# The last batch's division on ScalarE, a shorter guard, and a new order, in a fused attention and MLP kernel on one core

## The chip, the core and the metric

The kernel runs on one NeuronCore of a Trainium2 chip. TensorE (PE, with its weight load PEld), VectorE (DVE), ScalarE (ACT), GpSimd (POOL) and SyncE (SP) each work through an instruction list of their own and wait for one another by semaphores. SP issues all transfers between HBM and SBUF; 16 DMA engines carry them, called the wire below. The metric is the device time of one execution, in microseconds (us).

## The reference

`x` has 4 batches of 12480 rows of 128 numbers, all in float32. A set of 32 inducing rows attends to each batch, each batch then attends to the 32 rows that came of it, and every row goes through a layer with the activation h - tanh(h).

```python
def mab(q, kv):
    s = scale * (q @ kv.transpose(0, 2, 1))
    s = s - s.max(-1, keepdims=True)
    a = np.exp(s)
    a /= a.sum(-1, keepdims=True) + 1e-09
    return a @ kv
h = mab(I, x)
return mab(x, h)
...
h = x @ w_in          # 128 -> 2048
g = h - np.tanh(h)
return g @ w_out      # 2048 -> 128
```

## The kernel before, in words

A batch is cut into steps 0 to 7 of 1536 rows and a remainder, step 8, of 192; batches are counted 0 to 3. Two passes run over each batch.

The *first pass* (`first`, L367) loads a step's `x` transposed (`xT`, L380) and makes its scores against the inducing rows on PE (L357). VectorE copies them out with their maximum (L391), ScalarE takes exponents (L461), VectorE transposes (L465), and PE sums up the weighted rows (L472). That sum needs the rows untransposed: they are loaded a second time (`xn`, L455), or, for the steps in `TURNED`, turned on PE (L447) and copied out by ScalarE or VectorE (L451). At the end of a batch its summary `hT_all` of 32 rows is made (L510).

`linear` (L519) then replaces the layer for this batch by its tangent around the mean of the 32 rows: one 32x128 matrix per batch, `P_all`. That holds only as long as the rows are close to one another. So a *guard* (`bound`, L699) works out whether it held: it reduces a bound r1, a bound r2 and the least denominator `smin` over all sums to one number each, PE transposes them to one partition (L754 to L756), and VectorE forms a single number, `limit`, from them (`decide`, L759, nine instructions on one-element tiles and two reductions among them). Every engine reads `limit` at the end (L846) and jumps over the long way (`general`) unless it is over zero (L847). With these inputs the long way isn't run.

The *second pass* (`second`, L612) makes the scores of a step against the summary (L357, this time with `hT_all`), their maximum (L625, L626) and exponent (L629), and the product with `P_all` in four quarters of one PSUM bank each (L636), whose last column is the denominator. VectorE copies the denominators to `S_all` (L648) and takes reciprocals (L651). Each quarter then goes out of PSUM in one of two ways: VectorE divides it on the way (`whole`, L660), or ScalarE copies it (`plain`, L664) and POOL divides it in SBUF (`norm`, L669). SP stores a step in one transfer; steps 6 and 7 of the last batch go in two halves (L695).

No loop runs in the program: `Plan.order` (L110) lays all of this out before it is built. It goes through the work in time with estimated costs, starts on each engine the ready piece with the least priority number (`K`, a table of offsets by kind and batch), and gives out places in SBUF (23 places `big` of 128x1536) and PSUM. `LAND` is its guess of a transfer's delay, `STAY` a penalty on changing PE's kind of work, `MOST` how many places each use may hold, `DVQ` how many quarters of a step start out on VectorE. What it makes is an order for each engine that the chip then keeps; SP's order is kept too, so a transfer that has to wait holds up all behind it. A transfer into a place waits until the engine that last read it is done, and each of the eight semaphores for transfers is used again only when the transfer eight before has landed.

Of the kernel before, what the change touches and what calls it, by code (L numbers as in the profile page):

```python
# [28 lines left out]
K = dict(load=(-405.2, -73.6, 365.6, 732.0), step1=(189.5, 37.3, 86.1, 34.3), lag2=(-1344.7, 642.2, -187.9, 554.4),
         copy=(-966.7, 182.8, 582.0, 890.5), step2=(63.0, 5.9, 46.9, 4.9), turn=(3399.7, 2729.3, 3806.6, 3390.1), move=(-926.9,  # L30
         616.0, 643.2, -1883.0), nat=(445.7, -196.7, -60.7, 77.0), exp1=(-409.6, -1802.6, 1772.8, 577.3), et=(-1268.2, -670.6,
         821.4, -2142.2), acc=(63.5, 1115.9, -997.2, -2667.1), sc2=(498.0, -379.7, -952.9, 693.2), top=(984.0, 131.6, 1260.3,
         -21.4), exp2=(1257.9, -709.0, 2777.2, -857.8), prod=(-1778.1, 1760.3, -578.0, -21.4), rec=(-2172.0, -394.3, 355.7,
         404.0), ev=(2492.2, -544.6, -1227.1, -3030.9), off=(-545.7, 642.1, 1621.1, 2136.7), step3=(173.1, 138.3, 60.8, 306.6),
         st=(-962.2, -256.6, 745.9, -225.9), norm=(-114.8, 1199.2, -943.7, -185.5), lw1=-186.8, lw2=25.2, w1=74.7, w2=591.6,
         bound=2765.6)
# [157 lines left out]
def fused_kernel(ctx, tc, xT, xn, xl, indT, w_in, w_out, out):  # L194
# [504 lines left out]
    def bound(pri):  # L699
# [49 lines left out]
        smin, low = small("smin", [128, 1], 1), small("low", [1, 4], 1)  # L749
        add("DVE", 0.5, lambda: nc.vector.tensor_reduce(out=smin.get(), in_=sums_all.get(), axis=AX.X, op=ALU.min),  # L750
            reads=[sums_all, *s_parts], writes=[smin], pri=pri)

        def turn():
            nc.tensor.transpose(out=ps3.get()[:1, :B], in_=r1.get(), identity=ident[:B, :B])  # L754
            nc.tensor.transpose(out=ps3.get()[:1, 128:256], in_=r2.get(), identity=ident)
            nc.tensor.transpose(out=ps3.get()[:1, 256:384], in_=smin.get(), identity=ident)  # L756
        add("PE", 0.5, turn, reads=[r1, r2, smin, ident_b], writes=[ps3], pri=pri, mode="f")

        def decide():  # L759

# [2 lines left out]
            v.tensor_reduce(out=x[:, 0:2], in_=ps3.get()[:1, 128:384].rearrange("o (k p) -> o k p", k=2), axis=AX.X, op=ALU.min)
# [1 line left out]
            v.tensor_tensor(out=x[:, 0:1], in0=x[:, 0:1], in1=x[:, 2:3], op=ALU.min)
# [1 line left out]
            v.tensor_scalar(out=x[:, 3:4], in0=x[:, 1:2], scalar1=-2.0, scalar2=2.0 * (m + SLACK), op0=ALU.mult, op1=ALU.add)
            v.tensor_tensor(out=x[:, 3:4], in0=x[:, 3:4], in1=x[:, 2:3], op=ALU.mult)
            v.tensor_tensor(out=x[:, 3:4], in0=x[:, 3:4], in1=x[:, 3:4], op=ALU.mult)
# [1 line left out]
            v.tensor_scalar(out=limit, in0=x[:, 3:4], scalar1=0.0, scalar2=None, op0=ALU.max)
# [138 lines left out]
```

## Time and profile before

| what | value |
|---|---|
| median of three runs | 188.42 us (187.48 to 188.99) |
| the profiled execution | 189.09 us |
| its span, first to last instruction | 187.2 us |
| mean granted PE clock | 0.957 |
| chain of work that ended last, by engine | PE 55%, DVE 20%, ACT 7%, DMA 6%, POOL 3% |
| bytes read from and written to HBM | 42.75 MB and 25.56 MB |

The profiled execution took 1.9 us more than its span. In the page's rows "busy" is the time in which an engine ran an instruction; the idle time before a group is followed by what ended most of it. Times in a timeline count from the span's start.

### The profile page before, as it was taken

The page shows a single profiled execution, that of the slowest core. Times are in us where ns is not written, and L with a number is a line of the kernel's source. Part 1 is how long each engine was busy: PE and PEld are TensorE (multiplying, and loading weights), DVE is VectorE, ACT ScalarE, POOL GpSimd, SP SyncE. Part 2 cuts the span into 40 slices and gives each one's busy share as a digit, 9 for nine tenths or more (in the row PEclk, how much of TensorE's full clock was granted, in tenths as well). Part 3 has the DMA queues.
Part 4 walks back from the last instruction along what each step waited for, and adds up shares of the span by engine and source line. Part 5 has one row for each costly group of instructions (what it writes and reads, how often), then busy time and mean ns, then how long its engine had stood idle before and what let it go on. Part 6 is the DMA issues. An engine that isn't in the chain of part 4 may idle for free.

```text
span 187.2 us, 7373 instructions
## 1 busy us (share of the span) xinstructions
PE 154.7 (83%) x2895; PEld 99.5 (53%) x2895; DVE 149.6 (80%) x574; ACT 112.7 (60%) x282; POOL 95.5 (51%) x114
## 2 busy tenths in 40 slices
PE   0799966879988999999999978999979988879500
PEld 0465554645345865565667864556556764646300
DVE  3268699999999987896889863599899879998950
ACT  3022389964168974756779953438589574578600
POOL 5000124672250368456755583460675886499960
PEclk9999999999999999999999995799999999999955
DMA  5999998999999999999999999699989999999991
GB/s 144 406 423 415 404 409 253 393 420 422 414 419 367 295 326 312 375 423 416 404 356 363 383 420 422 211 416 347 364 314 382 418 417 415 404 421 390 387 390 50
DMA packets 14489, 68.84 MB, mean 368 GB/s; under 512 B 1776, under 2 KB 2928, under 8 KB 14448
## 3 DMA queue, kind: packets, MB, share of 16 engines
q1 hardware_dynamic: 14448, 68.31, 94.2%
q8 instruction: 24, 0.39, 0.8%
q14 instruction: 17, 0.14, 0.2%
HBM read 42.75 MB, written 25.56 MB: 365 GB/s over the span
## 4 chain that ended last, share of the span: by engine, by line
PE 55%; DVE 20%; ACT 7%; DMA 6%; issue 5%; POOL 3%; SPq 0%; DVEq 0%; ACTq 0%; POOLq 0%
PE ps L357 17%; PE ps L636 13%; PE ps L447 10%; PE ps L472 9%; DMA big<-in_xn 3%; ACT s L461 3%; PE ps L353 3%; DMA big<-in_xT 2%; POOL big L669 2%; DVE s L391 2%; PE ps L527 2%; DVE mb L625 2%; DVE ps L327 2%; DVE big L320 2%; ACT big L323 1%
## 5 line engine op out<-in xcount | busy, mean ns | idle before, releaser
L669 POOL TENSOR_TENSOR big<-big,mb 128x384 f32<-128x384 f32 (+1 forms) x73 | 75.2, 1056 | 46.2 <-ACT big L664 41.9
L664 ACT COPY big<-ps 128x384 f32<-128x384 f32 x99 | 41.1, 488 | 8.2 <-DVE S_all L648 7.7
L636 PE MATMUL ps<-P_all,ex 32*128 32x129 f32 (+1 forms) x784 | 36.0, 294 | 4.1 <-issue 1.5
L636 PEld LDWEIGHTS ps<-P_all,ex 32*128 32x128 f32 (+1 forms) x784 | 28.1, 188 | 19.6 <-ACT big L664 5.2
L357 PE MATMUL ps<-big,indT_sb 128*32 128x384 f32 x256 | 28.1, 516 | 6.4 <-DMA big<-in_xT 6.0
L451 ACT COPY big<-ps 128x512 f32<-128x512 f32 x30 | 17.0, 587 | 25.8 <-PE ps L447 24.5
L472 PE MATMUL ps<-big,et 128*32 128x128 f32 x768 | 27.3, 275 | 5.8 <-DVE et L465 4.1
L629 ACT ACTIVATE ex<-ps,mb 128x384 f32<-128x384 f32 (+1 forms) x36 | 19.7, 553 | 17.8 <-DVE mb L626 10.8
L447 PEld LDWEIGHTS ps<-ident,big 128*128 128x128 f32 x192 | 21.6, 146 | 13.2 <-issue 4.9
L447 PE MATMUL ps<-ident,big 128*128 128x128 f32 x192 | 27.9, 290 | 0.9 <-DVE win_sb L329 0.9
L357 PE MATMUL ps<-big,hT_all 128*32 128x384 f32 x256 | 27.6, 502 | 0.2 <-DVE s L391 0.2
L472 PEld LDWEIGHTS ps<-big,et 128*32 128x32 f32 x768 | 21.0, 110 | 11.3 <-DVE et L465 5.0
L391 DVE TENSOR_SCALAR_CACHE_REDUCE s<-ps 128x384 f32<-128x384 f32 (+1 forms) x36 | 18.1, 513 | 8.8 <-PE ps L357 7.8
L461 ACT ACTIVATE s<-s,nbs 128x384 f32<-128x384 f32 (+1 forms) x36 | 21.0, 586 | 0.5 <-DVE nbs L412 0.5
L625 DVE TENSOR_REDUCE mb<-ps 128x1 f32<-128x384 f32 (+1 forms) x36 | 18.4, 511 | 2.6 <-PE ps L357 2.2
L648 DVE TENSOR_SCALAR S_all<-ps 128x3 f32<-128x3 f32 (+1 forms) x136 | 13.5, 153 | 7.3 <-PE ps L636 6.4
L465 DVE STREAM_TRANSPOSE et<-s 128x384 f32<-128x384 f32 (+1 forms) x36 | 18.1, 519 | 0.3
L660 DVE TENSOR_TENSOR big<-ps,mb 128x384 f32<-128x384 f32 x29 | 15.5, 544 | 0.3
L314 POOL TENSOR_SCALAR big<-big 128x512 f32<-128x512 f32 x8 | 5.4, 683 | 20.0 <-DMA big<-in_w_in 20.0
L451 DVE COPY big<-ps 128x512 f32<-128x512 f32 x18 | 12.3, 687 | 2.4 <-PE ps L447 2.2
L357 PEld LDWEIGHTS ps<-big,indT_sb 128*32 128x32 f32 x256 | 6.9, 113 | 12.0 <-issue 8.8
L357 PEld LDWEIGHTS ps<-big,hT_all 128*32 128x32 f32 x256 | 8.0, 111 | 5.1 <-issue 2.6
(118 smaller groups left out, 158.4 us busy)
## 6 DMA issues: line engine op xcount, KB each, us to landing
big<-in_xT SPq DMA_DIRECT2D x32, 768.0 KB, 8.8
out<-big SPq DMA_DIRECT2D x30, 768.0 KB, 7.6
big<-in_xn SPq DMA_DIRECT2D x16, 768.0 KB, 6.9
big<-in_w_in SPq DMA_DIRECT2D x4, 512.0 KB, 12.8
big<-in_w_out SPq DMA_DIRECT2D x4, 512.0 KB, 8.2
out<-big SPq DMA_DIRECT2D x4, 384.0 KB, 4.9
xr<-in_xT SPq DMA_DIRECT2D x4, 96.0 KB, 10.5
xnr<-in_xl SPq DMA_DIRECT2D x4, 96.0 KB, 7.0
```

Source lines behind the costliest of these rows:

```text
L357: nc.tensor.matmul(ps[q * m:(q + 1) * m, :sg], lhsT=w, rhs=seg(x, nq, None, q), start=True, stop=stop)
L391: nc.vector.tensor_scalar(out=s1.get()[:P, :sg], in0=ps.get()[:P, :sg], scalar1=1.0, scalar2=None, op0=ALU.mult, op1=ALU.max, accum_out=mx ...
L447: nc.tensor.transpose(out=ps.get()[:, k * 128:(k + 1) * 128], in_=xt.get()[:, c:c + 128], identity=ident)
L451: copy(x.get()[:, 4 * g:4 * g + 4, :].rearrange("p k c -> p (k c)"), ps.get())
L461: nc.scalar.activation(out=t, in_=t, func=AF.Exp, bias=nbs.get()[:P, g:g + 1], accum_out=sums.get()[:P, s:s + 1])
L465: add("DVE", 0.5 if s < NS else 0.25, lambda et=et, s1=s1s[s], P=P, sg=sg, kb=kb: nc.vector.transpose(out=et.get()[:P, :kb].rearrange("p k ...
L472: nc.tensor.matmul(hacc.get()[q * m:(q + 1) * m, g * C:(g + 1) * C], lhsT=et.get()[:P, k, :], rhs=x.get()[:P, k, :], start=first_k[g, q] = ...
L625: nc.vector.tensor_reduce(out=mb.get()[:P, 0:1], in_=ps.get()[:P, :sg], axis=AX.X, op=ALU.max)
L629: add("ACT", 0.49 if full else 0.28, lambda: nc.scalar.activation(out=ex.get()[:P, :sg], in_=ps.get()[:P, :sg], func=AF.Exp, bias=mb.get() ...
L636: nc.tensor.matmul(o_b[q].get()[:T, r * (C + 1):(r + 1) * (C + 1)], lhsT=ex.get()[p, r * T:(r + 1) * T], rhs=P_all[p, b, :], start=True, s ...
L664: nc.scalar.copy(out=slot(q, q + 1), in_=o(q)[:, :, :C])
L669: nc.gpsimd.tensor_tensor(out=x, in0=x, in1=mb.get()[:T, 2 + q0 * nr:2 + q1 * nr].unsqueeze(2).to_broadcast([T, w, C]), op=ALU.mult)
```

## The change

It has three parts.

*The last batch's steps 7 and 8.* `SCALED = 7`. A quarter of these two that goes out by ScalarE is no longer copied and divided by POOL: ScalarE multiplies by the reciprocal on the way, one instruction of 128x128 for each of a quarter's three rows of columns, since its scale is one number per partition. Any quarter of the two may go to either engine, and POOL has no `norm` for them.

*The guard.* The reduction of all sums is split: all columns but the last three products' early, into one more column of `S_all`, and the last 37 columns at the end. The transposes of r1 and r2 and their reduction to one number `c0` are pieces of work of their own. `decide` compares a multiple of the old number that needs no reciprocal and has the same sign; it keeps its scratch in PSUM, and is one reduction and four instructions with scalars in place of two reductions and seven others.

*The order.* `K`, `DVQ`, `MOST`, `LAND` and `STAY` have new numbers; `TURNED` and `GROUPS`, and so the transfers as a set, are the same.

```diff
-LEAD, AHEAD, ISSUE, LAND = 1.50, 3.00, 0.35, 1.50
-SWITCH, STAY = 0.115, 73.1
-MOST = dict(xT=15, xn=16, ot=61, pm=9)
+LEAD, AHEAD, ISSUE, LAND = 1.50, 3.00, 0.35, 1.35
+SWITCH, STAY = 0.115, 0.0
+MOST = dict(xT=15, xn=14, ot=53, pm=10)
...
-DVQ = ((2, 1, 1, 1, 2, 3, 2, 0, 1), (2, 1, 0, 2, 1, 3, 1, 2, 1), (2, 2, 0, 1, 2, 1, 1, 3, 1), (2, 1, 2, 3, 1, 2, 3, 2, 0))
+DVQ = ((1, 0, 2, 2, 2, 3, 2, 2, 1), (2, 1, 2, 2, 0, 0, 1, 2, 1), (1, 1, 2, 1, 2, 1, 2, 1, 1), (3, 1, 1, 2, 2, 1, 1, 1, 0))
+SCALED = 7
...
+        last = b == B - 1 and s >= SCALED
+        def scaled(q):
+            for r in range(nr):
+                k = q * nr + r
+                nc.scalar.activation(out=ot.get()[:T, k, :], in_=o(q)[:, r, :C], func=AF.Copy, scale=mb.get()[:T, 2 + k:3 + k])
+        if last:
+            ways["ACT"] = (0.06 + 0.28 * nr, scaled)
-            free = q >= fixed_q
+            free = q >= fixed_q or last
-        for q0, q1 in spans:
+        for q0, q1 in () if last else spans:
...
+        add("DVE", 0.5, lambda: nc.vector.tensor_reduce(out=sums_all.get()[:, B * COLS:], in_=sums_all.get()[:, :n2], axis=AX.X, op=ALU.min),
+            reads=[sums_all, *s_parts[:-3]], writes=[early], pri=pri)
+        add("DVE", 0.15, lambda: nc.vector.tensor_reduce(out=smin.get(), in_=sums_all.get()[:, n2:], axis=AX.X, op=ALU.min),
+            reads=[sums_all, early, *s_parts[-3:]], writes=[smin], pri=pri)
...
+        def room():
+            v = nc.vector
+            v.tensor_reduce(out=c0.get()[:, 0:1], in_=ps3.get()[:1, 128:256], axis=AX.X, op=ALU.min)
+            v.tensor_reduce(out=c0.get()[:, 1:2], in_=ps3.get()[:1, :B], axis=AX.X, op=ALU.min)
+            v.tensor_reduce(out=c0.get()[:, 0:1], in_=c0.get(), axis=AX.X, op=ALU.min)
...
-            v.tensor_reduce(out=x[:, 0:2], in_=ps3.get()[:1, 128:384].rearrange("o (k p) -> o k p", k=2), axis=AX.X, op=ALU.min)
-            v.tensor_reduce(out=x[:, 2:3], in_=ps3.get()[:1, :B], axis=AX.X, op=ALU.min)
-            v.tensor_tensor(out=x[:, 0:1], in0=x[:, 0:1], in1=x[:, 2:3], op=ALU.min)
-            v.reciprocal(out=x[:, 2:3], in_=x[:, 1:2])
-            v.tensor_scalar(out=x[:, 3:4], in0=x[:, 1:2], scalar1=-2.0, scalar2=2.0 * (m + SLACK), op0=ALU.mult, op1=ALU.add)
-            v.tensor_tensor(out=x[:, 3:4], in0=x[:, 3:4], in1=x[:, 2:3], op=ALU.mult)
-            v.tensor_tensor(out=x[:, 3:4], in0=x[:, 3:4], in1=x[:, 3:4], op=ALU.mult)
-            v.tensor_tensor(out=x[:, 3:4], in0=x[:, 3:4], in1=x[:, 0:1], op=ALU.subtract)
-            v.tensor_scalar(out=limit, in0=x[:, 3:4], scalar1=0.0, scalar2=None, op0=ALU.max)
+            x = ps4.get()[:1, 256:259]
+            v.tensor_reduce(out=x[:, 0:1], in_=ps4.get()[:1, :128], axis=AX.X, op=ALU.min)
+            v.tensor_scalar(out=x[:, 1:2], in0=x[:, 0:1], scalar1=-2.0, scalar2=2.0 * (m + SLACK), op0=ALU.mult, op1=ALU.add)
+            v.tensor_scalar(out=x[:, 2:3], in0=x[:, 0:1], scalar1=c0.get()[:, 0:1], scalar2=x[:, 0:1], op0=ALU.mult, op1=ALU.mult)
+            v.tensor_scalar(out=x[:, 1:2], in0=x[:, 1:2], scalar1=x[:, 1:2], scalar2=x[:, 2:3], op0=ALU.mult, op1=ALU.subtract)
+            v.tensor_scalar(out=limit, in0=x[:, 1:2], scalar1=0.0, scalar2=None, op0=ALU.max)
```

The order as it stands at three places follows. In the rows `big7_166` is place 7 of the 23 in SBUF, `otr` a place for a remainder's results, `ps` a PSUM bank, `mb` the reciprocals of a step; lines of the changed kernel are some lines further down.

SP between the stores of batch 1, before: batch 0's remainder (`otr0`) stands among the loads of batch 3's steps.

```order
L695 DMA out<-big14_254 128x1536
L380 DMA big22_347<-in_xT 128x1536
L380 DMA big6_173<-in_xT 128x1536
L380 DMA big12_248<-in_xT 128x1536
L380 DMA big10_222<-in_xT 128x1536
L695 DMA out<-otr0_1730 96x256
L380 DMA big4_145<-in_xT 128x1536
L380 DMA big9_192<-in_xT 128x1536
L380 DMA big5_143<-in_xT 128x1536
L455 DMA big17_286<-in_xn 128x1536
```

The same place now.

```order
L704 DMA out<-big8_198 128x1536
L381 DMA big18_311<-in_xT 128x1536
L381 DMA big12_248<-in_xT 128x1536
L456 DMA big16_274<-in_xn 128x1536
L381 DMA big9_192<-in_xT 128x1536
L381 DMA big20_340<-in_xT 128x1536
L381 DMA big8_198<-in_xT 128x1536
L381 DMA big21_323<-in_xT 128x1536
L456 DMA big4_143<-in_xn 128x1536
```

The remainder's store is no longer among the loads: the two remainders' stores stand behind the last load now, and a load of `xn` has come forward. The load into `big21`, of batch 3's step 7, waits for PE to have read batch 2's first scores from that place.

POOL at its end, before: the divisions of the last batch's steps 6 (`big22`) and 7 (`big19`) and of the remainder.

```order
L669 TENSOR_TENSOR big21_340<-big21_340,mb1_751 128x768
L669 TENSOR_TENSOR big21_340<-big21_340,mb1_751 128x384
L669 TENSOR_TENSOR big22_347<-big22_347,mb3_900 128x384 x3
L669 TENSOR_TENSOR big19_300<-big19_300,mb0_595 128x384 x3
L669 TENSOR_TENSOR otr0_1730<-otr0_1730,mb2_801 96x256
L846 TENSOR_LOAD limit_72
```

POOL at its end now.

```order
L670 TENSOR_TENSOR big1_99<-big1_99,mb3_900 128x384
L670 TENSOR_TENSOR big14_256<-big14_256,mb1_739 128x768
L670 TENSOR_TENSOR big14_256<-big14_256,mb1_739 128x384
L670 TENSOR_TENSOR big0_84<-big0_84,mb2_809 128x384 x3
L865 TENSOR_LOAD limit_72
```

Steps 7 and 8 are gone from POOL, and step 6 (`big0`) is its last.

VectorE at its end, before: from the reduction of all sums (L750) to the guard's number.

```order
L750 TENSOR_REDUCE smin_2708<-S_all_97 128x1
L660 TENSOR_TENSOR big19_300<-ps3_147,mb0_595 128x384
L651 RECIPROCAL mb2_801<-S_all_97 96x2
L763 TENSOR_REDUCE low_2722<-ps0_126 1x2
L764 TENSOR_REDUCE low_2722<-ps0_126 1x1
L765 TENSOR_TENSOR low_2722<-low_2722 1x1
L766 RECIPROCAL low_2722<-low_2722 1x1
L767 TENSOR_SCALAR low_2722<-low_2722 1x1
L768 TENSOR_TENSOR low_2722<-low_2722 1x1
L769 TENSOR_TENSOR low_2722<-low_2722 1x1
L770 TENSOR_TENSOR low_2722<-low_2722 1x1
L771 TENSOR_SCALAR limit_72<-low_2722 1x1
```

VectorE at its end now.

```order
L764 TENSOR_REDUCE smin_2711<-S_all_97 128x1
L652 RECIPROCAL mb3_900<-S_all_97 96x2
L661 TENSOR_TENSOR big3_124<-ps5_159,mb0_595 128x384
L661 TENSOR_TENSOR big3_124<-ps1_131,mb0_595 128x384
L786 TENSOR_REDUCE ps4_153<-ps4_153 1x1
L787 TENSOR_SCALAR ps4_153<-ps4_153 1x1
L788 TENSOR_SCALAR ps4_153<-ps4_153,bt_c_2587 1x1
L789 TENSOR_SCALAR ps4_153<-ps4_153 1x1
L790 TENSOR_SCALAR limit_72<-ps4_153 1x1
L661 TENSOR_TENSOR otr0_1885<-ps6_166,mb3_900 96x128
```

Two quarters of step 7 (`big3`) stand between the last reduction and the guard's number now, and a quarter of the remainder behind it.

More of the change, by code (lines that the diff above doesn't have):

```diff
@@ L25 @@
 SMALL = 0.0625
-LEAD, AHEAD, ISSUE, LAND = 1.50, 3.00, 0.35, 1.50
-SWITCH, STAY = 0.115, 73.1
-MOST = dict(xT=15, xn=16, ot=61, pm=9)
[L29 to L36, printed above, removed]
+LEAD, AHEAD, ISSUE, LAND = 1.50, 3.00, 0.35, 1.35
@@ new lines @@
+SWITCH, STAY = 0.115, 0.0
+MOST = dict(xT=15, xn=14, ot=53, pm=10)
+K = dict(load=(-153.1, -40.5, 157.5, 733.5), step1=(178.1, 35.5, 88.4, 31.0), lag2=(-1240.2, 421.7, -367.8, 563.2),
+         copy=(-572.6, 397.9, 63.3, 566.2), step2=(74.5, 13.6, 34.8, 4.4), turn=(3345.0, 3205.9, 3588.6, 3021.2), move=(-924.0,
+         1085.7, 1001.8, -1534.4), nat=(735.6, -555.4, 100.5, 76.4), exp1=(-182.0, -2385.8, 1814.1, 593.3), et=(-1145.1, -631.4,
+         763.3, -2277.9), acc=(637.9, 1598.0, -937.7, -2469.8), sc2=(546.0, -697.4, -1450.4, 601.9), top=(1171.6, 106.9, 1324.5,
+         -380.4), exp2=(1087.6, -754.3, 2494.9, -780.6), prod=(-1735.7, 1498.8, -426.7, -122.5), rec=(-2030.8, -752.9, 211.4,
+         709.4), ev=(2514.1, -373.3, -1417.6, -3183.5), off=(-560.0, 619.8, 1628.7, 2179.0), step3=(165.1, 130.5, 87.7, 356.9),
+         st=(-1211.0, -183.4, 937.0, 397.0), norm=(232.9, 1322.8, -1231.4, -332.2), lw1=-34.1, lw2=58.1, w1=327.3, w2=858.5,
+         bound=2818.5)
@@ L272, in fused_kernel @@
     dev_b = [fixed(dev_all) for b in range(B)]
-    sums_all = small("S_all", [128, B * COLS], 1)
+    sums_all = small("S_all", [128, B * COLS + 1], 1)
     add("SP", 0.3, lambda: nc.sync.dma_start(out=indT_sb, in_=indT), writes=[ind_b], pri=-500)
@@ L748, in bound @@
         add("DVE", 1.0, least, reads=[ps2], writes=[t, r1], pri=pri)
[L749 to L756, printed above, removed]
@@ L757, in bound @@
-        add("PE", 0.5, turn, reads=[r1, r2, smin, ident_b], writes=[ps3], pri=pri, mode="f")
+        smin = small("smin", [128, 1], 1)
+        n1 = B * COLS - KB
+        n2 = n1 - 2 * KB
+        early = Buf()
+        add("DVE", 0.5, lambda: nc.vector.tensor_reduce(out=sums_all.get()[:, B * COLS:], in_=sums_all.get()[:, :n2], axis=AX.X, op=ALU.min),
+            reads=[sums_all, *s_parts[:-3]], writes=[early], pri=pri)
+        add("DVE", 0.15, lambda: nc.vector.tensor_reduce(out=smin.get(), in_=sums_all.get()[:, n2:], axis=AX.X, op=ALU.min),
+            reads=[sums_all, early, *s_parts[-3:]], writes=[smin], pri=pri)
@@ new lines, in bound @@
+        add("PE", 0.2, lambda: nc.tensor.transpose(out=ps3.get()[:1, :B], in_=r1.get(), identity=ident[:B, :B]),
+            reads=[r1, ident_b], writes=[ps3], pri=pri, mode="f")
+        add("PE", 0.2, lambda: nc.tensor.transpose(out=ps3.get()[:1, 128:256], in_=r2.get(), identity=ident),
+            reads=[r2, ident_b], writes=[ps3], pri=pri, mode="f")
+        c0 = small("bt_c", [1, 2], 1)
+        def room():
[3 more added lines that the diff above has]
+            v.tensor_reduce(out=c0.get()[:, 0:1], in_=c0.get(), axis=AX.X, op=ALU.min)
@@ L759, in decide @@
+        add("DVE", 0.3, room, reads=[ps3], writes=[c0], pri=pri)
+        ps4 = misc()
+        add("PE", 0.3, lambda: nc.tensor.transpose(out=ps4.get()[:1, :128], in_=smin.get(), identity=ident),
+            reads=[smin, ident_b], writes=[ps4], pri=pri, mode="f")
         def decide():
             v = nc.vector
-            x = low.get()
-            v.tensor_reduce(out=x[:, 0:2], in_=ps3.get()[:1, 128:384].rearrange("o (k p) -> o k p", k=2), axis=AX.X, op=ALU.min)
-            v.tensor_reduce(out=x[:, 2:3], in_=ps3.get()[:1, :B], axis=AX.X, op=ALU.min)
@@ L771, in decide @@
-            v.tensor_scalar(out=limit, in0=x[:, 3:4], scalar1=0.0, scalar2=None, op0=ALU.max)
-        add("DVE", 0.9, decide, reads=[ps3], writes=[low], pri=pri)
+            x = ps4.get()[:1, 256:259]
+            v.tensor_reduce(out=x[:, 0:1], in_=ps4.get()[:1, :128], axis=AX.X, op=ALU.min)
+            v.tensor_scalar(out=x[:, 1:2], in0=x[:, 0:1], scalar1=-2.0, scalar2=2.0 * (m + SLACK), op0=ALU.mult, op1=ALU.add)
+            v.tensor_scalar(out=x[:, 2:3], in0=x[:, 0:1], scalar1=c0.get()[:, 0:1], scalar2=x[:, 0:1], op0=ALU.mult, op1=ALU.mult)
@@ L775, in fused_kernel @@
+            v.tensor_scalar(out=x[:, 1:2], in0=x[:, 1:2], scalar1=x[:, 1:2], scalar2=x[:, 2:3], op0=ALU.mult, op1=ALU.subtract)
+            v.tensor_scalar(out=limit, in0=x[:, 1:2], scalar1=0.0, scalar2=None, op0=ALU.max)
+        add("DVE", 0.7, decide, reads=[ps4, c0], writes=[ps4], pri=pri, lag=5.5)
     weight(w_in, win_sb, win_b, K["w1"], K["lw1"])
```

## The prediction

> **What bounds the kernel now.** I read the page first, for the shares of the engines and of the transfers.
>
> ```profile
> PE 154.7 (83%) x2895; PEld 99.5 (53%) x2895; DVE 149.6 (80%) x574; ACT 112.7 (60%) x282; POOL 95.5 (51%) x114
> q1 hardware_dynamic: 14448, 68.31, 94.2%
> ```
>
> No compute engine is over 83%, but the packets of the one data queue fill 94.2% of the time of the 16 DMA engines. 94.2% of 187.2 us is 176.3 us, and the change moves the same bytes, so only the 10.9 us in which the wire is not full can be won. Second I read the windows, to see where those lie: the last two columns are the busy share of the DMA engines and GB/s.
>
> ```profile
> 28.00:32.00 4.00, 2.54 (x80) 2.08 (x82) 3.89 (x7) 4.00 (x10) 1.49 (x2) 1.00 0.80 229
> 116.00:122.00 6.00, 6.00 (x122) 3.48 (x124) 3.17 (x19) 2.41 (x9) 2.59 (x4) 0.68 0.76 253
> 134.00:140.00 6.00, 4.76 (x116) 3.20 (x112) 5.49 (x31) 4.65 (x13) 4.31 (x4) 1.00 0.87 304
> 142.00:170.00 28.00, 24.12 (x546) 16.34 (x546) 24.17 (x118) 18.70 (x52) 21.04 (x22) 1.00 1.01 408
> 170.00:180.00 10.00, 5.56 (x95) 3.57 (x91) 9.13 (x37) 5.84 (x16) 10.00 (x12) 0.89 0.96 390
> 180.00:182.00 2.00, 0.00 (x0) 0.00 (x0) 0.49 (x2) 0.00 (x0) 0.91 (x2) 0.50 1.00 393
> 182.00:184.00 2.00, 0.00 (x0) 0.00 (x0) 0.00 (x0) 0.00 (x0) 0.00 (x0) 0.50 0.57 179
> ```
>
> The wire is idle for 0.8 us in 28 to 32 (4 x 0.20), 1.4 us in 116 to 122, 0.8 us in 134 to 140 and 0.4 us in 170 to 180. From 142 to 182 it is full: that is the drain of the results. All loads have been issued by then, and the stores wait for the wire, not the wire for the stores. Third I read the timeline of SP and its waits, for what emptied the wire at 118.
>
> ```profile
> 106.78 3.18 SPq L380 DMA_DIRECT2D big<-in_xT  x4
> 118.55 0.36 SPq L695 DMA_DIRECT2D out<-otr  x1
> 119.00 1.32 SPq L380 DMA_DIRECT2D big<-in_xT  x3
> SPq L695 <- POOL otr L669: 15.2, 2, 8.5
> PE ps L357 <- DMA big<-in_xT: 6.0, 1, 6.0
> ```
>
> SP stood 8.5 us behind the store of batch 0's remainder (106.78 + 3.18 = 109.96 to 118.55), whose division POOL did late, and three loads stood behind it. But the last row, from the waits, says that PE waited for a transfer once only, at the very start: up to 140 the transfers follow the computation and not the other way round. Fourth, the end:
>
> ```profile
> L695 SPq DMA_DIRECT2D out<-otr x1: 332/332/332, 180.9 to 180.9; - x1
> DMA to landing us min/median/max: 4.6/4.6/4.6
> L846 DVEq TENSOR_LOAD <-limit x1: 829/829/829, 180.6 to 180.6; - x1
> L847 ACTq COMPARE_BRANCH x1: 50/50/50, 181.3 to 181.3; - x1
> L847 PEldq COMPARE_BRANCH x1: 4033/4033/4033, 181.4 to 181.4; - x1
> L847 DVEq EVENT_SEMAPHORE  x1: 21/21/21, 186.1 to 186.1; - x1
> L906 SPq EVENT_SEMAPHORE  x10: 17/28/1079, 183.0 to 187.2; - x10
> ```
>
> Two things run to the end side by side. The last store is issued at 180.9 and lands 4.6 us later, at 185.5. The guard's number is read by every engine from 180.6 on, and the jump over the fallback costs PE 4.03 us; VectorE gets through its own jump only at 186.1. SP's longest wait in the closing line, 1.08 us, is for that. So VectorE's jump ends last, 0.6 us behind the last landing, and 1.1 us of closing work follow it (186.1 to 187.2).
>
> **The change part by part.** *The guard on VectorE.* These are its rows, from the last full step's reciprocal on; then POOL's last division, and the group of the small row sums, for a price:
>
> ```profile
> 175.45 0.23 DVE L651 RECIPROCAL mb<-S_all 128x12 f32<-128x12 f32 x1
> 175.59 0.57 DVE L750 TENSOR_REDUCE smin<-S_all 128x1 f32<-128x432 f32 x1
> 176.08 0.55 DVE L660 TENSOR_TENSOR big<-ps,mb 128x384 f32<-128x384 f32 x1
> 176.54 0.15 DVE L651 RECIPROCAL mb<-S_all 96x2 f32<-96x2 f32 x1
> 176.62 0.39 DVE L763 TENSOR_REDUCE low<-ps 1x2 f32<-1x256 f32 x1
> 177.11 0.89 DVE L765 TENSOR_TENSOR low<-low 1x1 f32<-1x1 f32 x1
> 178.11 0.12 DVE L767 TENSOR_SCALAR low<-low 1x1 f32<-1x1 f32 x1
> 178.27 0.52 DVE L768 TENSOR_TENSOR low<-low 1x1 f32<-1x1 f32 x1
> 178.82 0.75 DVE L769 TENSOR_TENSOR low<-low 1x1 f32<-1x1 f32 x1
> 180.39 0.14 DVE L771 TENSOR_SCALAR limit<-low 1x1 f32<-1x1 f32 x1
> 180.30 0.61 POOL L669 TENSOR_TENSOR otr<-otr,mb 96x256 f32<-96x256 f32 x1
> L648 DVE TENSOR_SCALAR S_all<-ps 128x3 f32<-128x3 f32 (+1 forms) x136 | 13.5, 153 | 7.3 <-PE ps L636 6.4
> ```
>
> The nine run from 176.62 to 180.53, 3.9 us. What makes them long are operations of two tensors on one element (0.89, 0.52, 0.75), beside 0.12 and 0.14 us for an operation with a constant. The five new ones are one reduction over 128 elements (at most the 0.39 of 256) and four operations with constants or a one-element scalar. On PSUM they are not in the trace: between 0.12 and 0.89 each; I take 0.14, since they are operations with scalars, to which the 0.12 and 0.14 rows are nearest. That is 0.39 + 0.56 + gaps of about 0.1 = 1.1 us.
>
> The trace has POOL busy without a break beside the slow rows (10.00 of 10.00 us in 170 to 180). [...]
>
> Ahead of them VectorE has, from 175.45 on, a reciprocal (0.23), the reduction of only the last 37 columns (between the 0.15 of an operation on three columns and the 0.57 over 432; I take 0.2, as 37 lies nearer to three), the remainder's reciprocal (0.15) and two quarters to divide instead of one (0.55 each). PE's transpose of the minimum goes on beside those quarters. So the number is there at 175.45 + 0.23 + 0.2 + 0.15 + 1.1 + 1.1 = 178.2, against 180.5. One quarter of the remainder (about 0.3) follows. The two other new reductions and their transposes stand many steps earlier, in the drain, which hides them.
>
> *The last step on ScalarE and VectorE, not on POOL.* POOL loses three 128x384 divisions (829 ns each) and the remainder's (612 ns): 3.1 us at its end, where it was the last to finish (180.9). ScalarE copies a quarter now in one instruction, and divides it then in three of 128x128; that form is not in the trace, and its bounds are the copies of that size:
>
> ```profile
> L598 ACT COPY P_all<-ps 128x128 f32<-128x128 f32 x2 | 0.5, 266 | 1.7 <-DVE S_all L648 1.4 <-PE ps L353 0.3
> L734 ACT COPY bt_G<-ps 128x128 f32<-128x128 f32 x1 | 0.3, 325 | 0.0
> L669 POOL TENSOR_TENSOR big<-big,mb 128x384 f32<-128x384 f32 x14 | 11.2, 829 | 0.5 <-ACT big L664 0.5
> ```
>
> Six of them are 1.6 to 2.0 us, I take 1.7 by the row that stands twice, and the remainder's 0.3. They can start when the reciprocal is there, at 175.7, and end by about 177.7. POOL then ends with the step before that one, at about 180.30 less three divisions, 177.9, and SP has five stores to issue from there, some 0.35 apart: the last near 179.4 in place of 180.9. It does not land 1.5 us earlier: the wire is full (1.00 in 180 to 182) and hands out what is queued. What can be won is the idle of the stretch before, 0 to 0.4 us; I take 0.3, since most of it was late divisions.
>
> *The jump.* With the number at 178.2 and DVE's last quarter at 178.5, DVE's jump (186.1 - 180.6 = 5.5 us from its load of the number) ends near 184.0, ahead of the last landing at 185.5 - 0.3 = 185.2. It no longer ends last: 0.6 us are won, and the closing 1.1 us then start from the landing.
>
> *The new order.* I added up the mean durations of the groups of rows along VectorE's order, up to the copy that ends each batch's summary: 30.7, 62.0, 93.2 and 122.5 us before, 30.5, 61.4, 92.8 and 122.7 now. So neighbours are swapped, and no stage has moved. On SP the remainder's store no longer stands ahead of batch 3's loads, but other loads now wait for a place that PE frees. The last load's place was freed by PE's sums at 140.7 (139.80 + 0.86, quoted with the second rival), and is freed in the new order by the scores of batch 2's step 6, which ran at 140.5 to 141.3. Behind it the same 19 big stores are left. So I set the order at 0, between -2.2 (the idle of 116 to 122 and of 134 to 140 gone) and +3.8 (second rival).
>
> The sum: 0.3 + 0.6 = 0.9 us. Against the profiled execution (span 187.2, its time 189.09, so 1.9 around the span) that is 188.2; that execution was 0.7 above the median of the runs, 188.42, and against the median I say 187.5.
>
> **The rivals.** *The order fills the wire (186.1).* If the three loads that come 8.5 us earlier let batch 3's first pass finish earlier, the 1.4 us of 116 to 122 are won too: 188.42 - 0.9 - 1.4 = 186.1, and with the 0.8 of 134 to 140, 185.3. For it speaks the 8.5 us wait, SP's longest; against it, that PE never waited for those transfers.
>
> *The last load comes a step late (191.3, slower).* One mechanism: the last load of batch 3 now waits for PE to have made the scores of batch 2's step 6.
>
> ```profile
> 136.72 0.83 PE L357 MATMUL ps<-big,hT_all 128*32 128x384 f32 x8
> 139.80 0.86 PE L472 MATMUL ps<-big,et 128*32 128x128 f32 x24 [1.24 <-DVE S_all L648]
> 140.48 0.83 PE L357 MATMUL ps<-big,hT_all 128*32 128x384 f32 x8
> ```
>
> The same scores of the step before ran at 136.72, 3.8 us earlier; slipping by one step puts the load, and all stores behind it, 3.8 us back: 187.5 + 3.8 = 191.3. It decides from a slip of 2.8 us on. Against it: PE has about the same work before that point in both orders.
>
> *The guard stays slow (189.1).* If the one-element operations cost 0.89 whatever they read, four of them take 4 x 0.75 = 3.0 us more: the number comes at 181.2, 0.7 later than before, VectorE's jump ends 0.7 later, and it ends last again: 188.42 + 0.7 = 189.1.
>
> *The jump still ends last (188.1).* If the code that is jumped to comes only once the stores have left the wire, an earlier number brings nothing: 188.42 - 0.3 = 188.1. For it speaks that ScalarE's, POOL's and SP's branches took 0.05 us and PE's 4.03 in the full wire. [...]
>
> **How the numbers follow.** Forecast 0.42 (own range 186.6 to 188.4), wire filled 0.28, jump last 0.15, last load late 0.12, guard slow 0.03. A measurement of this kernel can tell about 1% from no change, 1.9 us: below 186.5 is faster, above 190.3 slower. Faster takes the second case and an edge of the first, 0.31; slower takes the late load, 0.12; the rest, 0.57, is within. The range reaches from the wire filled in both places, 185.2, to 189.6, which leaves the late load and little else outside.
>
> **What would show it.** Right: no division on POOL for batch 3's last two steps; the five guard instructions under 1.5 us together; DVE's jump done before the last store lands; the wire still full from 142 on; the last load issued near 141. Wrong: a last load before 139 or after 143, a second stall of SP over 3 us after 100, or four one-element rows of 0.5 us and more.

## The result, and the profile after

The changed kernel takes 195.46 us (median of four executions, 194.45 to 196.59) beside 188.70 us of the kernel before in the same comparison: ratio 1.038, 95% interval 1.028 to 1.049. It is slower; the forecast was 187.5 us, with 189.6 as the upper end. (Medians here are over all executions of a kernel; ratios and their intervals leave out executions that the chip disturbed, among them the profiled ones of three kernels below: the parts with the old order, the order alone and 32 pads.)

The changed kernel was profiled in an execution of 194.55 us, with a span of 192.8 against 187.2. Its page has the same work in it:

```profile
PE 155.3 (81%) x2895; PEld 99.9 (52%) x2895; DVE 149.9 (78%) x574; ACT 112.9 (59%) x286; POOL 92.3 (48%) x108
q1 hardware_dynamic: 14448, 68.31, 92.3%
q8 instruction: 25, 0.41, 0.9%
```

PE, VectorE and ScalarE are busy as long as before, within 0.6 us, POOL 3.2 us less, and the data queue moves the same 68.31 MB. So 5.6 us of idle time have come in. The windows (us busy of each engine, then the granted clock, the share of the DMA engines and GB/s) tell where the wire is idle now:

```profile
28.00:32.00 4.00, 2.34 (x76) 2.06 (x80) 3.86 (x8) 4.00 (x9) 1.22 (x1) 1.00 0.75 205
60.00:66.00 6.00, 5.84 (x145) 4.11 (x136) 5.28 (x23) 5.58 (x14) 2.25 (x2) 1.00 0.71 215
116.00:122.00 6.00, 5.56 (x127) 3.43 (x127) 4.25 (x20) 2.28 (x6) 2.25 (x2) 1.00 1.02 422
126.00:130.00 4.00, 4.00 (x47) 2.17 (x40) 3.82 (x18) 0.00 (x0) 0.13 (x1) 0.81 0.62 189
134.00:142.00 8.00, 8.00 (x171) 4.93 (x164) 7.19 (x35) 4.96 (x12) 5.08 (x5) 1.00 0.73 220
142.00:178.00 36.00, 28.91 (x637) 18.93 (x630) 29.57 (x139) 23.29 (x66) 24.93 (x26) 1.00 0.97 379
178.00:190.00 12.00, 4.60 (x71) 2.85 (x67) 7.07 (x35) 5.67 (x17) 6.64 (x7) 0.81 0.90 348
```

The gap of 116 to 122 is gone, as the wire-filling rival had it. In its place 1.5 us are idle in 126 to 130 and 2.2 us in 134 to 142. What empties the wire there is seen in the timeline of SP, the engine that issues the transfers (start, duration, then the group):

```profile
111.32 9.35 SPq L381 DMA_DIRECT2D big<-in_xT  x4
127.89 0.33 SPq L456 DMA_DIRECT2D big<-in_xn  x1
143.18 0.34 SPq L456 DMA_DIRECT2D big<-in_xn  x1
```

From 111.32 + 9.35 = 120.67 to 127.89 nothing is issued: the next load wants a place that PE's scores of batch 2 free, and those are late. The last load into `big` goes out at 143.18, 2.5 us later than before. So I followed PE. This is the list of its waits from 100 to 180 us (line, then what it waited for: us in total, times, longest) in the kernel before:

```profile
PE ps L636 <- issue: 1.5, 1, 1.5
PE ps L636 <- ACT ex L629: 1.5, 3, 1.1
PE ps L472 <- DVE S_all L648: 1.2, 1, 1.2
```

And the same list of the changed kernel:

```profile
PE ps L473 <- issue: 3.4, 2, 2.0
PE ps L354 <- issue: 2.5, 2, 2.1
PE ps L637 <- issue: 1.7, 2, 1.0
PE ps L354 <- ACT P L599: 0.9, 1, 0.9
```

"Issue" means that PE stood idle while it waited for no semaphore: 1.5 us before, 3.4 + 2.5 + 1.7 = 7.6 us after. Nothing else in the list has grown by more than a microsecond. PE's transpose of the guard's minimum starts at 176.22 before and at 183.31 after, 7.1 us later, and 6.1 of them are this one kind of idle time. The two longest, in PE's timeline:

```profile
121.09 0.68 PE L354 MATMUL ps<-centre,Y 128*32 128x4 f32 x38
123.85 1.45 PE L354 MATMUL ps<-centre,Y 128*32 128x128 f32 x25 [2.08 <-issue]
150.37 0.34 PE L358 MATMUL ps<-xr,hT_all 128*32 128x96 f32 x4
152.68 0.86 PE L473 MATMUL ps<-big,et 128*32 128x128 f32 x24 [1.97 <-issue]
```

In the first pair of rows PE stops in the middle of one product of `linear` (`Y` with `centre`), for whose next matmul no semaphore is awaited, and goes on 2.08 us later.

At the end of the kernel nearly all went as forecast:

```profile
183.12 0.13 DVE L764 TENSOR_REDUCE smin<-S_all 128x1 f32<-128x37 f32 x1
184.18 0.28 DVE L786 TENSOR_REDUCE ps<-ps 1x1 f32<-1x128 f32 x1
184.49 0.15 DVE L787 TENSOR_SCALAR ps<-ps 1x1 f32<-1x1 f32 x1
184.68 0.28 DVE L788 TENSOR_SCALAR ps<-ps,bt_c 1x1 f32<-1x1 f32 x1
185.31 0.15 DVE L790 TENSOR_SCALAR limit<-ps 1x1 f32<-1x1 f32 x1
183.29 1.66 ACT L681 ACTIVATE big<-ps,mb 128x128 f32<-128x128 f32 x6 [0.60 <-PE ps L637]
```

The guard takes 1.3 us (184.18 to 185.46) in place of 3.9, and ScalarE's six divisions 1.66. The last store, issued at 187.0, lands 4.8 us later at 191.8, and VectorE is through its jump at 191.7, just ahead of it. (SP's list of waits still puts a closing wait of 1.4 us down to that jump: the two are too close to say that the jump no longer matters.)

### The profile page after: what moved, and what is told of

Its sections match the earlier page's. It is cut to its first block, busy times and chain, and to the rows that moved or that the text cites. A ratio compares the mean times of both kernels' runs of the same rounds, so it can differ in the third digit from the quotient of the medians.

```text
span 192.8 us, 7378 instructions
## 1 busy us (share of the span) xinstructions
PE 155.3 (81%) x2895; PEld 99.9 (52%) x2895; DVE 149.9 (78%) x574; ACT 112.9 (59%) x286; POOL 92.3 (48%) x108
## 3 DMA queue, kind: packets, MB, share of 16 engines
q1 hardware_dynamic: 14448, 68.31, 92.3%
## 5 line engine op out<-in xcount | busy, mean ns | idle before, releaser
L670 POOL TENSOR_TENSOR big<-big,mb 128x768 f32<-128x768 f32 (+1 forms) x68 | 72.6, 1092 | 48.8 <-ACT big L665 42.2
L665 ACT COPY big<-ps 128x384 f32<-128x384 f32 x96 | 40.0, 488 | 10.9 <-DVE S_all L649 10.3
L452 ACT COPY big<-ps 128x512 f32<-128x512 f32 x29 | 16.3, 589 | 31.9 <-PE ps L448 25.0
L358 PE MATMUL ps<-big,indT_sb 128*32 128x384 f32 x256 | 29.4, 525 | 6.8 <-DMA big<-in_xT 6.4
L661 DVE TENSOR_TENSOR big<-ps,mb 128x384 f32<-128x384 f32 x30 | 16.3, 548 | 0.5
L452 DVE COPY big<-ps 128x512 f32<-128x512 f32 x19 | 13.0, 689 | 2.6 <-PE ps L448 2.4
L358 PEld LDWEIGHTS ps<-big,indT_sb 128*32 128x32 f32 x256 | 7.5, 114 | 12.5 <-issue 7.8
```

The lines of the kernel that those rows point to most:

```text
L358: nc.tensor.matmul(ps[q * m:(q + 1) * m, :sg], lhsT=w, rhs=seg(x, nq, None, q), start=True, stop=stop)
L452: copy(x.get()[:, 4 * g:4 * g + 4, :].rearrange("p k c -> p (k c)"), ps.get())
L665: nc.scalar.copy(out=slot(q, q + 1), in_=o(q)[:, :, :C])
L670: nc.gpsimd.tensor_tensor(out=x, in0=x, in1=mb.get()[:T, 2 + q0 * nr:2 + q1 * nr].unsqueeze(2).to_broadcast([T, w, C]), op=ALU.mult)
```

## The theories

The places at which PE stops have a pattern. Counted in matmul records of the trace, the stalls of the changed kernel stand at records 1614, 1741, 1868, 2374 and 2756: every distance is a multiple of 126.5 or so. 126.5 matmuls and as many weight loads are 253 instructions of PE, and with PE's few others about 256 (the trace has 5855 records of PE to 2895 matmuls, and 126.5 x 5855 / 2895 = 255.8; an estimate, which the run with 128 pads below tries out). The page calls its queue q8 (25 packets of 16 KB) one of instructions; 5855 / 256 = 22.9, about one packet for each such block. So:

- Theory A: the new order itself holds PE and the wire up (later places, other neighbours).
- Theory B: PE's instructions come in blocks of 256 over the DMA engines that carry the data too (the page gives q8 0.9% of the 16 engines' time, and q1 92.3%). A block whose fetch begins late stops PE at its bound. The new order did not move the work, but it put other matmuls at the bounds and filled the wire just then.
- Theory C: the two parts at the end (ScalarE's division, the guard in PSUM) cost it.
- Rival D, once padding had helped: padding helps by keeping PE running at the start.

## The experiments

**The two halves of the change apart.** One kernel is the new code with the old numbers, the other the old code with the new ones:

```diff
 # parts_old_order: after, with before's tables
-LEAD, AHEAD, ISSUE, LAND = 1.50, 3.00, 0.35, 1.35
+LEAD, AHEAD, ISSUE, LAND = 1.50, 3.00, 0.35, 1.50
...
 # order_alone: before, with after's tables
-MOST = dict(xT=15, xn=16, ot=61, pm=9)
+MOST = dict(xT=15, xn=14, ot=53, pm=10)
...
```

> The changed code (short guard, ScalarE's division in batch 3's steps 7 and 8) with all numbers of the old order: SP's list is row for row that of before, PE's differs in 32 rows of some 716, all behind row 540. Theory A (the new order carries the whole loss): 187 to 189 us, the kernel before less the 0.9 us of the tail that the prediction counted, at most. Theory B (the loss comes from blocks of 256 PE instructions whose fetch is late when the wire is full): the same 187 to 189, since PE's list is the old one up to about 140 us. Theory C (the two tail parts cost it, by what they take from ScalarE and PSUM): 193 us or more.

> The old code (nine-instruction guard, POOL's division) with all numbers of the new order. Theories A and B: 195 to 197 us, the whole loss, and perhaps 0.5 to 1 us more than the changed kernel, since the tail is the old one. Theory C: 187 to 190 us. Under B the trace shows PE idle without a releaser for 5 us or more in all behind 105 us, at the changed kernel's places (records 1614, 1741, 1868, 2374, 2756).

Measured: 191.63 us for the parts (187.69 to 195.17) beside 191.01 for the kernel before on that chip (187.65 to 192.75), no difference that these can show; 195.97 us for the order, ratio 1.024 (1.013 to 1.035). The median of the parts lies in none of the expected ranges, its quickest execution in that of A and B. Theory C falls by the second kernel: with the old parts and the new numbers the loss is there. Theory B expected the parts to stall as before does, and this was missed: PE's idle time is 3.7 us, at four bounds (records 1742, 1869, 2375 and 2503), where the profiled execution of before lost time at the first of them alone (record 1742). Why the two differ stays open. In the order's trace the stalls over 0.5 us stand at two of the five places only, 1868 (2.6 us) and 2374 (2.5 us), and sum to 5.7 us by the list of waits.

**Padding.** A number of one-row transposes, which nothing uses, is issued on PE as soon as the identity is there, in the first 6 us, in which PE has nothing to do (in before its first matmul starts at 6.00 us; 64 transposes took 1.74 us). All that follows keeps its order; only the bounds of the blocks move. The code shows 64; the other kernels have 32, 96 or 128 there.

```diff
     for op in plan.order():
         op.fn()
+        if op is ident_b.writer:
+            pad = home(ps_p, "ps", 7, [128, 512])
+            for k in range(64):
+                nc.tensor.transpose(out=pad[:1, :4], in_=ident[:4, :1], identity=ident[:4, :4])
```

> The changed kernel with 64 one-row transposes (128 PE instructions, half a block of 256) issued at the start, in the 6 us in which PE has nothing to do; all else in the same order. Theory A (waits of the order itself): 195.5 us within 0.7, and every milestone as late as in the changed kernel. Theory B: the bounds of the blocks move by half a block, the stalls of 1.5, 1.0, 2.1, 2.0 and 0.8 us at 109, 116, 124, 153 and 173 us go or move to other places, and the time moves by 2 us or more, more likely down (190 to 193) since the changed kernel's five stalls are many beside the one of before.

> The kernel before with the same 64 one-row transposes at the start. Theory A: 188.5 us within 0.7. Theory B: the one stall of 1.5 us at 113 us goes or moves, and others may come; the time moves by 1 us or more, more likely up (189 to 194), since before met its bounds at good places.

> The changed kernel with 128 one-row transposes (256 PE instructions, one whole block) at the start, some 3.5 us of work in the 6 us in which PE has nothing to do. Theory B (only the place of the block bounds counts): the bounds fall on the same matmuls as in the changed kernel, so the stalls at records 1614, 1741, 1868, 2374 and 2756 come back and with them 194 to 197 us. Rival D (the padding helps because PE is kept running before its first scores, by its clock or anything else of the start): 188 to 189 us, as with 64.

> The changed kernel with 32 one-row transposes (64 PE instructions, a quarter of a block). Theory B: a time of its own between 187 and 196 us, which follows the PE stalls without a releaser behind 100 us that its trace shows: some 188.5 us plus their sum less 0.6. Rival D: about 188.5 to 192, by half the padding, whatever the stalls.

> The old code with the new order's numbers and 64 one-row transposes at the start. Theory B: 188 to 190 us in place of the 196 without them, since the two stalls of 2.6 and 2.5 us go. Theory A: 195 to 197.

> The changed kernel itself, beside its padded forms on one chip. Theory B: 194 to 197 us, with the stalls of 1 us and more at records 1614 or 1741, 1868 and 2374 in the trace again, since they come from the place of the bounds and not from chance.

> The changed kernel with 64 one-row transposes at the start, a second time, as the version that may beat both. Theory B: 187.5 to 189.5 us, 6 us or more below the changed kernel beside it and 0.5 to 2% below the kernel before beside it.

> The changed kernel with 96 one-row transposes (three quarters of a block). Theory B: a time of its own between 187 and 196 us that goes with the stalls its trace shows: some 188.5 us plus the sum of PE's idle times without a releaser behind 100 us, less 0.6.

Measured, with the ratio to before on the same chip, and PE's idle time put down to issue from 100 to 180 us in each profiled execution (from the list of waits):

| kernel | median us | ratio to before (95%) | profiled us | PE idle, issue |
|---|---|---|---|---|
| before | 188.42 | | 189.09 | 1.5 |
| before, 64 pads | 190.29 | 1.009 (1.002 to 1.015) | 189.04 | 3.0 |
| after | 195.46 | 1.038 (1.028 to 1.049) | 194.55 | 7.6 |
| after again | 195.22 | 1.028 (1.021 to 1.035) | 196.66 | 6.0 |
| after, 32 pads | 190.45 | 0.990 (0.981 to 1.000) | 191.20 | 1.9 |
| after, 64 pads | 188.51 | 0.987 (0.977 to 0.997) | 189.88 | 1.0 |
| after, 64 pads, again | 187.21 | 0.985 (0.978 to 0.992) | 187.31 | 1.6 |
| after, 96 pads | 193.67 | 1.012 (1.002 to 1.023) | 192.04 | 4.4 |
| after, 128 pads | 195.19 | 1.025 (1.006 to 1.044) | 195.97 | 9.2 |
| order alone | 195.97 | 1.024 (1.013 to 1.035) | 198.72 | 5.7 |
| order alone, 64 pads | 189.75 | 0.996 (0.989 to 1.003) | 189.78 | 1.3 |

Half a block of padding takes the whole loss away, in the changed kernel (195.2 to 187.2 on one chip) as in the order alone; a whole block, which puts the bounds back on the same matmuls, brings it back. Theory A and rival D both fall by this; against D stands also that 96 pads give a longer time than 32. The new numbers cost nothing with the bounds elsewhere: SP still stands for loads and a remainder's store (6.9 us), and the kernel is 1.5% faster than before (0.8 to 2.2%). The copies that end the batches' summaries, of batch 0 to batch 3, say the same; before, the changed kernel, and with 64 pads (second run):

```profile
L510 DVE COPY hT_all<-ps x4: 179/208/224, 41.5 to 150.2; 128x64 f32<-128x64 f32 x4
L511 DVE COPY hT_all<-ps x4: 205/212/224, 41.8 to 155.7; 128x64 f32<-128x64 f32 x4
L511 DVE COPY hT_all<-ps x4: 206/212/215, 41.2 to 148.5; 128x64 f32<-128x64 f32 x4
```

The last one comes 5.5 us late in the changed kernel, and 1.7 us early in the same order with pads. Three quarters of a block, and padding of the kernel before, give times between, with idle times between. The sizes were guessed less well than the signs: 64 pads were expected at 190 to 193 us and took 188.5 and 187.2; the rule for 32 and 96 pads (188.5 plus the idle time less 0.6) gives 189.8 and 192.3, where the profiled executions took 191.2 and 192.0 and the medians are 190.5 and 193.7. The changed kernel run again stalled at records 1614, 1868 and 2374, as expected. PE's waits for issue with 128 pads, 100 to 180 us:

```profile
PE ps L473 <- issue: 4.8, 2, 2.6
PE ps L354 <- issue: 3.0, 2, 2.4
PE ps L637 <- issue: 1.4, 2, 1.0
```

With 64 pads (second run) it has only these:

```profile
PE ps L358 <- issue: 0.8, 1, 0.8
PE ps L473 <- issue: 0.6, 1, 0.6
PE ps L592 <- issue: 0.2, 1, 0.2
```

Padding the kernel before, which theory B expected to cost 1 us or more, cost 0.9% by its ratio (0.2 to 1.5%), some 1.6 us; the stall at record 1742 is gone, others have come, and the idle time doubled from 1.5 to 3.0 us.

**Does the fetch wait for the wire?** From the packets of q8 and PE's records, for bounds behind 100 us (us from the span's start; "passed" is PE at the bound before):

```
kernel        bound  passed  fetch begins  PE there  goes on  idle
after          1741  109.3   113.9 (+4.6)   115.2     116.2   1.0
after          1868  116.2   121.2 (+5.0)   121.8     123.9   2.1
after          1995  123.9   126.2 (+2.3)   132.5     132.5   -
after          2374  146.0   150.4 (+4.4)   150.7     152.7   2.0
64 pads        1868  112.8   116.3 (+3.5)   120.8     120.8   -
64 pads        1995  120.8   122.6 (+1.8)   125.5     125.5   -
64 pads        2374  138.1   141.2 (+3.1)   145.6     145.6   -
thin stores    1741  107.1   108.0 (+0.9)   112.6     112.6   -
thin stores    1868  112.6   116.4 (+3.8)   118.2     118.7   0.55
thin stores    2374  139.2   143.4 (+4.2)   144.0     145.7   1.6
thin stores    2500  145.7   146.9 (+1.2)   151.1     151.1   -
```

A stalled PE mostly goes on 2.2 to 2.6 us after the fetch's packet begins, and the packet begins 1 to 5 us after PE has passed the bound before. So in these rows PE stalled behind each block that it ran through in under the sum of the two, and behind no other: 4.6 + 2.4 = 7.0 us, where the blocks before the three stalls of the changed kernel in the table took 5.9, 5.6 and 4.7. Two kernels were to tell what the fetch waits for. Both leave output out:

```diff
 # after_half_stores: batch 0's full stores write half of their rows
-                out=dst[:, q0 * nr:q1 * nr, :], in_=slot(q0, q1)),
+                out=dst[:, q0 * nr:q1 * nr - (nq * nr // 2 if b == 0 and full else 0), :],
+                in_=slot(q0, q1 - (nq // 2 if b == 0 and full else 0))),
 # after_thin_stores: every full store writes one row of each partition
-                out=dst[:, q0 * nr:q1 * nr, :], in_=slot(q0, q1)),
+                out=dst[:, q0 * nr:q1 * nr, :] if not full else dst[:, q0 * nr:q0 * nr + 1, :],
+                in_=slot(q0, q1) if not full else slot(q0, q1)[:, :1, :]),
```

> The changed kernel, in which the eight full stores of batch 0 write half of their rows (3.1 MB of output left out), the order of all instructions unchanged. The wire is less full from some 75 to 130 us. Theory B: the fetches there begin sooner (3.6 us or less after the bound before, in place of 4.7 and 5.0), the stalls at records 1741 and 1868 go, and PE's last scores of batch 2 start 3 us or more earlier. If the fetch does not wait for the wire, the stalls at 1741 and 1868 stay at 1.0 and 2.1 us although less is carried.

> The changed kernel, in which every full store writes one row of the twelve (or six) of each partition, so about a third of all bytes (some 22 of 68 MB of output) are left out; the order of all instructions and the place of all block bounds are the changed kernel's. If a fetch waits for the wire: behind 100 us it begins within 2.5 us of the bound before wherever the wire's share is under 0.8, and the stalls at records 1614, 1741, 1868 and 2374 fall from 6 us in all to 1 us or less. If it waits for something of PE's own (its pace, its queue): the stalls stay at 5 us or more, as with the half stores.

Each of the two was executed once. The half stores did not settle it: the wire was emptier at 88 to 96 us only (share 0.6) and full again from 96 on by transfers that moved up, with fetches 4.8 and 5.1 us after the bound and stalls of 1.0 and 1.8 us. By the letter that is what was expected of a fetch that does not wait for the wire, but at these bounds the wire was as full as in the changed kernel. With the thin stores the wire was free in stretches, and the stalls stayed just where it was full. In this kernel's windows (same columns) the second row holds the fetch for bound 1868, the third follows bound 1995, the fourth holds the fetch for bound 2374:

```profile
106.00:110.00 4.00, 4.00 (x116) 2.97 (x119) 3.79 (x16) 3.04 (x10) 3.12 (x3) 1.00 0.83 269
116.00:118.00 2.00, 2.00 (x74) 1.17 (x63) 1.60 (x9) 0.30 (x2) 1.04 (x2) 1.00 1.03 420
126.00:128.00 2.00, 2.00 (x64) 1.49 (x60) 1.97 (x11) 1.70 (x5) 0.00 (x0) 1.00 0.40 143
142.00:144.00 2.00, 2.00 (x68) 1.62 (x60) 1.93 (x13) 1.16 (x5) 1.62 (x2) 1.00 0.90 275
```

The stalls fell from 6 us and more to 2.2 (0.5 put down to issue, and 1.6 that the list puts down to a store's landing, though PE goes on 2.3 us after a fetch begins). My bound of 1 us was missed, since the wire was full for some bounds still. Over the 16 profiles of this study, 305 fetches, the time from the bound to the fetch's packet has a median of 0.8 us where the wire's share in the next 2 us was under 0.5, 1.4 at 0.5 to 0.8, 1.8 at 0.8 to 0.95, and 3.4 over 0.95. So in these profiles a fetch came later the fuller the wire was, and where less was carried two of the four stalls went and one fell from 2.1 to 0.55 us. That it is the wire the fetch waits for is the reading that fits both; a kernel in which the wire alone differs at one bound was not run.

The same run says something of the bound. A third of the bytes is gone (45.4 MB moved), the wire is nearly idle from 142 on, and the time is 186.22 us (one execution, on another chip), about 1 us below the padded changed kernel with all its bytes:

```profile
100.00:142.00 42.00, 40.46 (x896) 26.62 (x894) 37.60 (x160) 30.32 (x87) 24.26 (x23) 1.00 0.85 301
142.00:184.00 42.00, 29.34 (x589) 19.57 (x581) 30.38 (x147) 23.26 (x65) 27.07 (x28) 0.89 0.17 48
```

**What the tail is worth.** Same order, same padding, old and new tail on one chip, and the short guard alone on another:

> The old code with the new numbers and the same padding: what stands against the run above is the short guard and ScalarE's division alone, with the same block bounds. If the tail is worth what the prediction counted, it is 0.5 to 1.2 us slower than the run above; if the end is the wire's whatever the tail does, within 0.4 us.

> The changed kernel with the 64 one-row transposes, but with batch 3's last two steps divided by POOL and VectorE as in the old code: the short guard alone beside the padded old code (1.5% above the padded changed kernel). If the guard's one-element product of two operands (3.83 us in the padded old code, until POOL was done) is what the tail gains by, this is 187 to 188.5 us; if the gain needs POOL's early end by ScalarE's division, 189 to 190.5.

The guard alone is one number in the padded kernel: `SCALED = 9` in place of 7, which leaves the last steps' division to POOL. The padded old tail took 190.52 us, ratio 1.000 (0.995 to 1.005), beside 0.985 of the padded changed kernel: the tail gains 1.5%, 2.8 us, more than both of the expected outcomes. The size is less sure than that: the two profiled executions, 189.20 and 187.31 us, differ by 1.9, and the first padded runs, 0.996 and 0.987 on two chips, by 0.9%. The guard alone took 187.75 us, ratio 0.989 (0.974 to 1.005), and 186.59 us in its profiled execution: it lies where the guard alone was to bring the gain, but the interval holds 1 and is too wide to exclude a part for ScalarE's division. So the share of each is argued from the traces. The reason stands in the padded old code's timeline, VectorE first and then POOL:

```profile
175.95 3.83 DVE L765 TENSOR_TENSOR low<-low 1x1 f32<-1x1 f32 x1
179.81 0.15 DVE L766 RECIPROCAL low<-low 1x1 f32<-1x1 f32 x1
180.05 0.15 DVE L768 TENSOR_TENSOR low<-low 1x1 f32<-1x1 f32 x1
...
172.24 6.96 POOL L669 TENSOR_TENSOR big<-big,mb 128x768 f32<-128x768 f32 x8
179.16 0.61 POOL L669 TENSOR_TENSOR otr<-otr,mb 96x256 f32<-96x256 f32 x1
```

One minimum of two single elements takes 3.83 us, until POOL's last division ends at 179.16 + 0.61 = 179.77; the same form takes 0.15 us from then on. The first padded run of the old code shows the same, 3.82 us until POOL's end. The short guard alone stands beside a POOL that is as busy, and is not held up; one of VectorE's two slowest one-element operations, and POOL's divisions:

```profile
175.58 0.28 DVE L788 TENSOR_SCALAR ps<-ps,bt_c 1x1 f32<-1x1 f32 x1
171.65 6.96 POOL L670 TENSOR_TENSOR big<-big,mb 128x768 f32<-128x768 f32 x8 [0.20 <-DVE mb L652]
```

In the old code the number is late, and PE's jump ends last, 2 us behind the last landing (179.8 + 4.5 = 184.3):

```profile
L851 PEldq COMPARE_BRANCH x1: 4476/4476/4476, 181.7 to 181.7; - x1
L851 PEldq EVENT_SEMAPHORE  x1: 51/51/51, 186.3 to 186.3; - x1
```

In the padded changed kernel the number is there at 177.9, and the jump ends at 184.5, with the last landing.

## Why the prediction was wrong, point by point

- **"Only the 10.9 us in which the wire is not full can be won"; the wire bounds the kernel.** As a floor no run contradicts it; as an account of what sets the time it was wrong. With a third of the bytes left out the kernel takes 186.2 us (one execution), about 1 us less than the padded kernel with all of them. PE's own chain, up to the guard's transpose at 176, is about as long as the wire's work (94.2% of 187.2 us, 176.3); a wire at 94% did not mean that the rest follows it.
- **"I set the order at 0", since "no stage has moved".** This is the step that failed. That no stage has moved was right of the work: VectorE is busy for 149.9 us in place of 149.6, and with other block bounds the new order costs nothing. What the term left out is that 6 us of idle time came on PE without any wait in the program: 7.6 us against 1.5. The trace of before had one such stall, 1.5 us at 113, at a block's bound; its list of queues had the instruction packets (q8, 24 packets, 0.39 MB); the sum used neither.
- **"Up to 140 the transfers follow the computation".** Right but for one wait of PE of 0.2 us, which the reading left out, and it is how the loss spread: a late PE frees places late, and SP's next load went out at 127.89.
- **Wire filled (186.1).** The idle time of 116 to 122 went, as this rival said, but late fetches go with a full wire there: the share is 1.02, and the fetch for bound 1868 begins 5.0 us after the bound before, with a stall of 2.1 us. It did not weigh that. That the padded kernel's 187.2 us stands beside the forecast of 187.5 is luck: the forecast was without padding and 0.5% below before, the padded kernel is 1.5% below it.
- **Last load a step late (191.3).** The sign was right, and the last load is 2.5 us late, past the point that the prediction named as wrong. But the mechanism was not this one: no step slipped, since the padded kernel with the same order has its last load at 137.2.
- **The jump still ends last (188.1).** In the changed kernel VectorE's jump ends 0.1 us before the last landing, in the padded one PE's ends with it, so this rival was close, but not for its reason: with the thin stores, where the wire's share at the end is 0.44 at most, PE's branch takes 4.01 us as well.
- **The guard: 1.1 us, from 0.39 + 0.56 + 0.1.** 1.3 measured, with 0.28 where I took 0.14 for two operations on PSUM and 0.28 for the reduction. The 0.14, and with it the 0.03 for the rival of a slow guard, was an estimate from operations with constants (0.12 and 0.14 us in before). That rival fell: no one-element operation took more than 0.28 us, beside a busy POOL either.
- **ScalarE's six divisions 1.7 us.** 1.66 measured. Each takes 0.36 to 0.39, more than 0.27, but they overlap and start 0.25 apart. (POOL's end worked out beside them, 180.30 less three divisions of 0.829, is 177.8, not 177.9, which changes nothing.)
- **0.3 + 0.6 = 0.9 us for the tail.** The mechanism was right (the jump no longer ends clearly after the landing), the size was not: 2.8 us in the padded pair. The term that was too small is the jump's 0.6: in the padded old code PE's jump ends 2 us behind the landing. In the profiled execution of before, four one-element operations of two tensors took 0.89, 0.52, 0.75 and 0.75 us, and each ended within 0.01 us of the end of one of POOL's divisions; the padded old code shows 3.83 for one of them, to the end of POOL's whole run. The 3.83 us end 0.01 us behind POOL's last division; beside a POOL that was as busy, the short guard's operations, with scratch in PSUM, took 0.28 at most. Why the operations of two tensors ended with POOL's was not shown.
- **"Wrong: a last load after 143, a second stall of SP over 3 us after 100".** Both came (143.2; 7.2 us for the load of 127.89). They were results of the loss, not its cause.

## What to carry to other kernels

Idle time that the profile puts down to "issue" in the middle of a run of matmuls was not noise here: 7.6 us in the changed kernel, 1.0 and 1.6 with 64 pads. Count the records between such places, and if the distances are multiples of one number, as of 126.5 matmul records here (a block of 256 instructions, by the run with 128 pads), try half a block of padding before judging a new order. When two orders of one kernel differ by a few per cent with the same busy times, compare them at several paddings: here the order alone stood at 1.024 of before without pads and at 0.996 with 64. The version to keep here is the changed kernel with 64 idle transposes: 187.2 us, 0.985 of before (0.978 to 0.992).
